# Attention with a token mixer: the last two heads' rows divided while turned, and first products of output blocks moved between the main loop, the ending and the tail

## The chip, the core and the metric

One core of one Trainium2 chip runs the whole program. Its engines are TensorE (PE, with PEld its weight loads), VectorE (DVE), ScalarE (ACT), GpSimd (POOL) and SyncE (SP, which only issues transfers here). The metric is the device time of one execution in microseconds (us), as the median of several runs.

## What is computed

Cut to what matters (`_layernorm`, `_silu`, `_gelu` as usual):

```
xn = layernorm(x)                       # x: 2048 tokens x 512
q, k, v = split(xn @ wqkv)              # 32 heads of 16
s = concat_heads(softmax(q k^T / 4) v) @ wo
h = layernorm(xn)
u = gelu(einsum("bsd,sf->bdf", h, w1) + b1)     # F = 1792
g = silu((einsum("bdf,fs->bds", u, w2) + b2)^T)
out = x + s * g
```

## The kernel before, in words

Matrix operands are kept as an upper and a lower part (`fp32r`), so one product of the reference is three matmuls: upper by upper, upper by lower, lower by upper (`three`, and the three entries in `products`, L1033). Below, "product" means one such matmul over 128 rows.

**Main loop.** After the projections, the loop at L1274 runs in steps of two units, s = 0, 2, ..., 534; NU = 512 and LEAD = 22. For s < 512 a step computes the row maxima of scores (`max_of`: 8 matmuls L532 into 3 PSUM banks, each followed by a VectorE reduction L536); 22 units later it computes the scores again (`score`: 8 matmuls L999, each followed by a ScalarE exponential L1004); two units after that `values` multiplies the probabilities by v (L1015), four heads' columns at a time. Every 16 units `max_rows` turns the maxima into two extra pieces of VectorE work (L551 and L548, L548), popped in the next two steps. Scores and maxima use only 48 or 50 rows of the array, on the lower or upper half of it; so every product that fills the gaps is cut into two halves of 64 rows (`halves`, L1144, matmuls at L1156) that run beside scores and maxima on the other half. How many products a step gets is set by `count` (L1167), and their place in it by `ORDERS` and `WIDE`, written out by hand.

The fill is one long generator: first `mixer` (14 blocks of 48 products with w1, then 16 blocks of 42 with w2), then `rest` (L1023). A mixer block of 42 is spread over eight steps: 6, 6, 5, 5, 5, 5, 5, 5 products; a block of 48 over nine: 6, 6, 6 and six of 5. For the one block whose index equals `SLOW` (4) the divisor is 15 and not 16, and what is left of it in the steady loop is taken as 5, 5, 5, 5, 5, 4, 4, 4. After the mixer, `rest` makes the attention's output products in first parts: for each block b of 128 tokens, nine products over head groups 0 to 2 (`range(ND - 1)`), for b < PARTS = 14. Such a block of nine takes two steps at once (`both_pairs`). Its sum is copied out by ScalarE (`part`, L922), multiplied by the gate g and added to x by GpSimd, and stored to DRAM (`y_d`).

**The ending** is the 12 steps from s = 512 on: no maxima are left, 22 more units of scores are. Scores and the former maxima's banks are one list of seven (L1281), the eighth is `values`'. A half step (`a_half`, L1184) takes up to three products; up to s = 522 only the first half of a step takes any (L1333). The products here are group 3's: three for each of blocks 8 to 13, then three for each of blocks 0 to 7. `finish` (L975) multiplies and adds on VectorE and, for blocks 0 to 7, stores the output. `own` (L831) treats heads 30 and 31 (the last pair), whose sums are never stored to DRAM: for the first 1024 tokens they are divided and moved by DMA into rows 96 to 127 of group 3's operand `oc[3, 0..1]`; `in_halves` reloads partial sums and gates into operands no longer needed, two per step, on SP's queue.

**The tail** is what follows the loop (L1368 on). Blocks 14 and 15 have all their products here, 12 each (`beside`, L1375, handed out by `some`). The last pair's sums of the second 1024 tokens are copied (`ev`, L724), turned by four transposes (L840), inverted (L843), spread wide (L845), turned back (L854), multiplied (L858), split (L859 and L94), and then multiplied with the rows of wo that belong to heads 30 and 31, laid out in a tile of their own (`load_last_w`, `split_last_w`): three products for each of blocks 8 to 15 (L101 to L103). `gated`, `added` and `in_parts` then multiply by the gate, add, and store each block.

Of the kernel before, what the change touches and what calls it, by code (L numbers as in the profile page):

```python
# [21 lines left out]
def tile_attention_token_mixer(ctx, tc, x, wqkv, wo, w1, b1, w2, b2, out):  # L22
# [746 lines left out]
    def divide(m, g, span):  # L769
# [61 lines left out]
    def own(span, ev):  # L831
        rq = sm.tile([P, 4, 4], F32, name="rq", bufs=1)
        wide = el.tile([P, 512], F32, name="t", bufs=4)

        def one(pl=ps_mx, nm="mx", spread=1):

            ps = pl.tile([P, 512], F32, name=nm)
# [6 lines left out]
            for k in range(0, 4, 4 // spread):  # L844
                nc.vector.tensor_copy(  # L845
                    wide.rearrange("p (k j r) -> p k j r", k=4, j=4)[:, k : k + 4 // spread],
                    rq[:, k : k + 4 // spread].unsqueeze(3).to_broadcast([P, 4 // spread, 4, 32]),
                )

        def two(pl=ps_mx, nm="mx", ks=range(4)):  # L850

            ps = pl.tile([P, 512], F32, name=nm)
            for k in ks:
                nc.tensor.transpose(ps[:, k * P : (k + 1) * P], wide[:, k * P : (k + 1) * P], ident)  # L854
            return ps

        def times(ps, of, at):
            nc.vector.tensor_tensor(out=ev[:, at], in0=ps[:, at], in1=ev[:, at], op=OP.mult)  # L858
            nc.scalar.copy(of[:, 0, at], ev[:, at])  # L859

        def lower(of, at):
            sub(nc.vector, of[:, 1, at], ev[:, at], of[:, 0, at])

        if span == QH - 1:
            asides.extend((one, two, times, lower))
            return

        def move_in():
            ps = two()
            of = el.tile([P, 2, 512], F32R, name="uo")  # L870
            times(ps, of, slice(0, 512))
            lower(of, slice(0, 512))
# [7 lines left out]


    last_w = {}

    def load_last_w():
        for c in range(2):
            raw = last_w[c] = wp.tile([P, 4, P], F32, name="raw", bufs=3).rearrange("p a b -> p (a b)")
            nc.gpsimd.memset(raw, 0.0)
            for a in range(2):
                row = 32 * (2 * a + c) + DH * a
                h = H - 2 + a  # L890
                nc.gpsimd.dma_start(raw[row : row + DH, :], wo[DH * h : DH * (h + 1), :])

    def split_last_w():
        for c in range(2):
            raw = last_w[c]
            w = last_w[c] = el.tile([P, 2, 512], F32R, name="uo")
            nc.scalar.copy(w[:, 0, :], raw)
            after(2 + 2 * c, lambda w=w, raw=raw: sub(nc.vector, w[:, 1, :], raw, w[:, 0, :]))


# [6 lines left out]
    PARTS = NB // 2 + 6  # L907
    blocks = list(range(NB // 2, PARTS)) + list(range(NB // 2))

# [39 lines left out]
    def load_out(n):  # L949
        b = blocks[n]  # L950
        y, g = (("xt", "gt"), ("u", "sq"))[n % 2]
        if b < NB // 2:
            ys[b] = el.tile([P, D], F32, name=y)
            nc.sync.dma_start(ys[b], y_d[b])
        gts[b] = el.tile([P, D], F32, name=g)
        nc.sync.dma_start(gts[b], g_d[b])
# [3 lines left out]
    def plan_halves():  # L960

        rows = [oc[g, c][:, m, :].bitcast(F32) for c in range(NC - 1) for g in range(ND - 1) for m in range(2)]
        own = PARTS - NB // 2
        for n in range(own, len(blocks) - 3):
            b = blocks[n]
            in_halves.extend(((ys, b, y_d[b]), (gts, b, g_d[b])))
# [8 lines left out]
    def finish(n, ps):  # L975
        b = blocks[n]
        half = PARTS - NB // 2 <= n < len(blocks) - 3
        r = el.tile([P, D], F32, name="t", bufs=4) if half else gts[b]
        nc.vector.tensor_tensor(out=r, in0=ps, in1=gts[b], op=OP.mult)
        o = ys[b] if b >= NB // 2 else r  # L980
        nc.vector.tensor_tensor(out=o, in0=ys[b], in1=r, op=OP.add)
        if b < NB // 2:
            nc.sync.dma_start(out[b * P : (b + 1) * P, :], r)
        if n + 3 < PARTS - NB // 2:
            load_out(n + 3)
        elif n < PARTS - NB // 2:
            load_out(n + len(blocks) - PARTS + NB // 2)
# [35 lines left out]
    def rest():  # L1023
# [20 lines left out]
        for b in range(PARTS):  # L1044
# [6 lines left out]
        yield from until(lambda: now[0] >= NU and (ND - 1, QH - 1) in divided)  # L1051
        for n in range(3):
            load_out(n)
        plan_halves()
        for n, b in enumerate(blocks):
            if b == 0:
                yield from until(lambda: own_done and (ND - 1, 0) in divided)
# [3 lines left out]
            yield lambda n=n, ps=ps: finish(n, ps), back  # L1061
# [28 lines left out]
    SLOW = 4  # L1090
# [76 lines left out]
    def count():  # L1167
# [10 lines left out]
        return min(6, -(-left // -(-3 * left // (15 if i == SLOW else 16)))) if left > 0 else 0  # L1178
# [95 lines left out]
    for s in range(0, total + 1, 2):  # L1274
# [53 lines left out]
        else:  # L1328


            for i in range(2):

                a_half(*(heads[a][1][2 * i : 2 * i + 2] for a in range(2)), i == 0 or s >= NU + 2 * (PARTS - NB // 2))  # L1333
# [89 lines left out]
    for k in range(5):  # L1423
        if k < 4:
            times(shares[k], of, cols[k])
# [46 lines left out]
```

## Time and profile before

| what | value |
|---|---|
| median of 3 runs | 1624.81 us (1624.67 to 1625.59) |
| the profiled execution: span from its first to its last instruction | 1622.0 us |
| time of the profiled execution around its span | not given; the median stands 2.8 us above the span |
| busy: PE, DVE, ACT, POOL | 1615.0, 1423.3, 1195.1, 561.6 us |

PE is TensorE; its ends are modelled, so "busy" for it is no proof that it is at its peak. A mean of 0.999 of TensorE's full clock was granted. Times in the trace are counted from the span's start: the main loop's steady part runs from about 203 to 1553 us, the ending to 1604, the tail to 1622.

### The profile page before, as it was taken

How to read it: one execution, taken by the hardware profiler on the slowest of the kernel's cores; microseconds unless marked ns; L12 is line 12 of the kernel's file. 1: busy time of each engine (PE TensorE's matmuls, PEld its weight loads, DVE VectorE, ACT ScalarE, POOL GpSimd, SP SyncE). 2: the span in 40 equal slices, each digit the busy share in tenths (PEclk: the TensorE clock that was granted, in tenths of full speed). 3: DMA queues.
4: the chain of work that ended last, by engine and by line, in shares of the span. 5: the costliest groups of instructions: out<-in, count | busy, mean ns of one | idle time of the engine just before them, and what ended most of it. 6: DMA issues, size and time to landing. Idle time of an engine off the chain costs nothing.

```text
span 1622.0 us, 31241 instructions
## 1 busy us (share of the span) xinstructions
PE 1615.0 (100%) x11937; PEld 877.2 (54%) x11937; DVE 1423.3 (88%) x2493; ACT 1195.1 (74%) x2311; POOL 561.6 (35%) x661
## 2 busy tenths in 40 slices
PE   9999999999999999999999999999999999999998
PEld 7888854544555544554554554545544544454544
DVE  7665999999999999999999999999999999999966
ACT  3333477777777777777877787777777778888885
POOL 1224844342244332342333332322222333642430
PEclk9999999999999999999999999999999999999999
DMA  7478441515133141826151522305151515444355
GB/s 237 181 242 204 114 92 41 95 41 75 41 70 73 30 82 34 241 70 108 41 86 38 82 65 40 77 22 76 38 85 37 112 39 84 123 101 130 106 192 192
DMA packets 152402, 155.60 MB, mean 96 GB/s; under 512 B 51564, under 2 KB 110188, under 8 KB 149180
## 3 DMA queue, kind: packets, MB, share of 16 engines
q1 hardware_dynamic: 147964, 152.87, 38.9%
q8 instruction: 94, 1.54, 0.4%
q0 software_dynamic: 4288, 0.73, 0.3%
q14 instruction: 56, 0.46, 0.1%
HBM read 101.86 MB, written 50.58 MB: 94 GB/s over the span
## 4 chain that ended last, share of the span: by engine, by line
PE 98%; DVE 1%; ACT 1%; DMA 0%; SPq 0%; issue 0%; POOL 0%; DVEq 0%
PE av L1015 31%; PE dn L1156 25%; PE sc L999 16%; PE mx L532 13%; PE sc L435 3%; PE dn L671 3%; PE mx L435 2%; PE av L435 1%; PE sc L101 0%; PE sc L103 0%; PE sc L102 0%; ACT prob L1004 0%; DVE mxp L536 0%; PE mx L999 0%; PE dn L1200 0%; PE mx L103 0%
## 5 line engine op out<-in xcount | busy, mean ns | idle before, releaser
L536 DVE TENSOR_REDUCE mxp<-mx 128x1 f32<-128x512 f32 x2026 | 1250.1, 680 | 116.1 <-PE mx L532 85.0
L1004 ACT ACTIVATE prob<-sc 128x512 f32<-128x512 f32 x2004 | 1040.4, 606 | 282.3 <-PE sc L999 117.6
L532 PE MATMUL mx<-big 48*128 48x512 f32 x2026 | 771.1, 418 | 0.1
L999 PE MATMUL sc<-big 50*128 50x512 f32 x2004 | 734.5, 411 | 0.0
L1015 PE MATMUL av<-prob,vp 128*32 128x512 f32 x4096 | 545.6, 604 | 0.3 <-DVE ev L722 0.2
L1156 PE MATMUL dn<-hu,wh 64*128 64x512 f32 x1520 | 508.0, 404 | 0.0
L999 PEld LDWEIGHTS sc<-big 50*128 50x128 f32 x2004 | 355.6, 186 | 230.0 <-ACT prob L1004 205.2
L532 PEld LDWEIGHTS mx<-big 48*128 48x128 f32 x2026 | 356.9, 185 | 187.7 <-DVE mxp L536 168.7
L1156 PEld LDWEIGHTS dn<-hu,wh 64*128 64x128 f32 x1520 | 271.8, 184 | 74.3 <-issue 49.5
L1156 PE MATMUL dn<-hu,wl 64*128 64x512 f32 x762 | 302.4, 397 | 0.0
L1015 PEld LDWEIGHTS av<-prob,vp 128*32 128x32 f32 x4096 | 80.9, 108 | 177.3 <-issue 165.0
L94 POOL TENSOR_TENSOR wl<-raw,wh 128x512 fp32r<-128x512 f32 x124 | 150.9, 1219 | 60.5 <-ACT wh L166 26.9
L1156 PEld LDWEIGHTS dn<-hu,wl 64*128 64x128 f32 x762 | 140.5, 184 | 12.6
L164 POOL CAST wh<-raw 128x512 fp32r<-128x512 f32 x104 | 60.6, 583 | 196.0 <-PE mx L532 76.0
L560 POOL CAST m<-f 16x128 fp32r<-16x128 f32 x31 | 8.7, 280 | 304.0 <-DVE f L548 303.9
L98 POOL DMA_DIRECT2D big<-m x124 | 65.8, 537 | 0.0
L1156 PE MATMUL dn<-wh,hu 64*128 64x512 f32 x168 | 59.7, 408 | 0.0
L621 POOL TENSOR_TENSOR sq<-u 128x512 f32<-128x512 f32 x11 | 11.5, 1041 | 133.8 <-ACT u L615 133.7
L708 POOL TENSOR_SCALAR t<-t 128x512 f32<-128x512 f32 x16 | 23.8, 1489 | 83.4 <-ACT t L705 83.4
L435 PE MATMUL sc<-xt,big 128*128 128x512 f32 x184 | 44.3, 389 | 0.0
L94 POOL TENSOR_TENSOR hu<-hx,hu 128x512 fp32r<-128x512 f32 x16 | 20.4, 1294 | 67.7 <-ACT hu L278 67.7
L671 PE MATMUL dn<-hu,wh 64*128 64x512 f32 x128 | 42.3, 392 | 0.0
(235 smaller groups left out, 1214.9 us busy)
## 6 DMA issues: line engine op xcount, KB each, us to landing
raw<-in_B_w_dram SPq DMA_DIRECT2D x104, 256.0 KB
big<-k_d SPq DMA_DIRECT2D x96, 128.0 KB
big<-q_d SPq DMA_DIRECT2D x96, 128.0 KB
q_d<-sg SPq DMA_DIRECT2D x16, 512.0 KB
k_d<-sg SPq DMA_DIRECT2D x16, 512.0 KB
num_d<-ev SPq DMA_DIRECT2D x30, 256.0 KB
u_d<-uo SPq DMA_DIRECT2D x14, 512.0 KB
hu<-u_d SPq DMA_DIRECT2D x14, 512.0 KB
```

The lines of the kernel that those rows point to most:

```text
L94: eng.tensor_tensor(out=o, in0=a, in1=b.bitcast(F32), op=OP.subtract)
L98: queue.dma_start(dst.bitcast(F32), src.bitcast(F32))
L164: nc.gpsimd.tensor_copy(whs[n][:, :m, :], raws[n][:, :m, :])
L435: nc.tensor.matmul(ps, w[part][:, kd, m], xt[kd][:, z, :], start=w is wh and z == 0 and kd == 0, stop=w is wl and kd == ND - 1,)
L532: nc.tensor.matmul(ps, q[o : o + 48, r * P : (r + 1) * P], k[o : o + 48, c * 512 : (c + 1) * 512], start=True, stop=True,)
L536: nc.vector.tensor_reduce(mxp[u // 16][:, a, r % 8, c : c + 1], ps, axis=AX.X, op=OP.max)
L671: nc.tensor.matmul(ps, w(slice(0, 64)), m(slice(0, 64)), start=first, stop=last)
L708: nc.gpsimd.tensor_scalar(t, t, 1.0, None, op0=OP.add)
L999: nc.tensor.matmul(ps, ks[p][o : o + 50, kb * P : (kb + 1) * P], qs[p][o : o + 50, at : at + 512], start=True, stop=True,)
L1004: nc.scalar.activation(e, ps, AF.Exp, scale=scale)
L1015: nc.tensor.matmul(av[32 * j : 32 * j + 32, :], vps[p][:, kb, 16 * a : 16 * a + 32], prob.pop((t, a, c)), start=kb == 0, stop=kb == NB - 1,)
L1156: made.append(lambda r=r, start=first and a == lead, stop=last and a != lead: nc.tensor.matmul(ps, w(r), m(r), start=start, stop=stop,))
```

## The change

Four things, all in one diff:

1. Blocks 11 and 12 have their nine first products in the ending (interleaved by group: three of block 11, three of block 12, and so on), in the half steps in which blocks 8 to 13 had their three products of group 3. `PARTS` becomes 13, and blocks 13, 14 and 15 have their nine first products in the tail. Blocks 0 to 10 stay in the main loop.
2. Six mixer blocks of w2 (indices 16, 18, ..., 26) get the divisor 15 too: they are spread over nine steps, 5, 5, 5, 5, 5, 5, 4, 4, 4.
3. In the tail, the last pair's rows are divided right after the first turn, while tokens lie on partitions (four multiplications of 128 x 64 into a cleared tile), turned back in four pairs of transposes straight to rows 96 to 127, and written by ScalarE (upper) and VectorE (lower), 32 x 256 each, into rows 96 to 127 of group 3's operand. Group 3 then needs three products for each of blocks 8 to 15, with all 128 rows and the ordinary weights; the special weight tiles, their loads on GpSimd's queue and their splits go.
4. `finish` serves blocks 0 to 7 only; the rows 96 to 127 of the operands are no longer cleared in `divide`, and one tile is cleared at s = 528 instead.

The diff, cut to its core:

```diff
@@ own @@
         if last:
             for c in range(2):
                 made.append(hu.tile([P, 2, 512], F32R, name="hu"))
-                nc.gpsimd.memset(made[c][DH * n :, :, :].bitcast(F32), 0.0)
...
     def own(span, ev):
+        if span == QH - 1:
+            asides.append(ev)
+            return
...
-    def load_last_w():
-    def split_last_w():
...
+    apart = []
+    def clear_apart():
+        apart.append(el.tile([P, 2, 512], F32, name="uo"))
+        nc.gpsimd.memset(apart[0], 0.0)
...
-    PARTS = NB // 2 + 6
-    blocks = list(range(NB // 2, PARTS)) + list(range(NB // 2))
+    PARTS = NB - 3
+    LATE = NB - 5
+    HALVES = 5
...
-    def finish(n, ps):
+    def finish(b, ps):
+        r = el.tile([P, D], F32, name="t", bufs=4) if b < HALVES else gts[b]
         nc.vector.tensor_tensor(out=r, in0=ps, in1=gts[b], op=OP.mult)
+        nc.vector.tensor_tensor(out=r, in0=ys[b], in1=r, op=OP.add)
+        nc.sync.dma_start(out[b * P : (b + 1) * P, :], r)
+        if b + HALVES < NB // 2:
+            load_out(b + HALVES)
...
+        def whole_part(b):
             yield from until(lambda: all((g, b // (NB // QH)) in divided for g in range(ND - 1)))
             ps, back = ps_sc.hold("dn")
             ps = ps[:, :D]
             yield from products(ps, b, range(ND - 1))
             yield lambda b=b, ps=ps: part(b, ps), back
             yield None
-        yield from until(lambda: now[0] >= NU and (ND - 1, QH - 1) in divided)
-        for n in range(3):
-            load_out(n)
+        for b in range(LATE):
+            yield from whole_part(b)
+        yield from until(lambda: now[0] >= NU)
         plan_halves()
-        for n, b in enumerate(blocks):
+        late = [whole_part(b) for b in range(LATE, PARTS)]
+        for n in range(ND - 1):
+            for turn in late:
+                yield from (itertools.islice(turn, 3) if n < ND - 2 else turn)
+        yield from until(lambda: own_done and (ND - 1, 0) in divided)
+        for b in range(NB // 2):
...
-    SLOW = 4
+    SLOW = (4, 16, 18, 20, 22, 24, 26)
...
-        return min(6, -(-left // -(-3 * left // (15 if i == SLOW else 16)))) if left > 0 else 0
+        return min(6, -(-left // -(-3 * left // (15 if i in SLOW else 16)))) if left > 0 else 0
...
-            if s == NU + 4:
-                load_last_w()
+            if s == NU + 16:
+                clear_apart()
...
-            if s == total - 6:
-                split_last_w()
...
     for b in range(PARTS, NB):
         sums[b] = ps_sc.hold("dn")[0][:, :D]
-        for g in range(ND):
+        for g in range(ND - 1):
...
+    some(3)
+    turned = ps_sc.tile([P, 512], F32, name="sc")
+    for k in range(4):
+        nc.tensor.transpose(turned[:, cols[k]], ev[:, cols[k]], ident)
+    some(3)
+    turned = turned.rearrange("p (k j r) -> p k j r", k=4, j=4)
+    for a in range(2):
+        nc.vector.reciprocal(rq[:, :, 2 * a : 2 * a + 2], turned[:, :, 2 * a : 2 * a + 2, 16 - 16 * a])
+    for c in range(2):
+        for a in range(2):
+            j = 2 * a + c
+            nc.vector.tensor_tensor(
+                out=spread[:, c, :, 96 + DH * a : 112 + DH * a], in0=turned[:, :, j, DH * a : DH * a + DH],
+                in1=rq[:, :, j].unsqueeze(2).to_broadcast([P, 4, DH]), op=OP.mult,
+            )
+    back = [ps_sc.tile([P, 512], F32, name="sc") for h in range(2)]
+    def turn_back(h, c):
+        for k in range(2):
+            at = slice((2 * c + k) * P, (2 * c + k + 1) * P)
+            nc.tensor.transpose(back[h][:, at], spread[:, c, 2 * h + k, :], ident)
+    def upper(h, c):
+        nc.scalar.copy(oc[ND - 1, 2 + c][96:, 0, 256 * h : 256 * h + 256], back[h][96:, 256 * c : 256 * c + 256])
+    def lower(h, c):
+        o = oc[ND - 1, 2 + c][96:, :, 256 * h : 256 * h + 256]
+        sub(nc.vector, o[:, 1, :], back[h][96:, 256 * c : 256 * c + 256], o[:, 0, :])
+    half = [NB // 2 + i for i in (0, 1, 4, 2, 3, 5, 6, 7)]
...
+    turn_back(0, 0)
+    some(1)
+    turn_back(0, 1)
+    some(2)
+    for c in range(2):
+        upper(0, c)
+        lower(0, c)
+    product(0)
+    product(1)
+    for c in range(2):
+        turn_back(1, c)
+        upper(1, c)
+    adding = {0: [0], 1: [], 2: [1], 3: [3, 2], 4: [], 5: [5, 4], 6: [6]}
+    for n, more in enumerate((0, 0, 2, 2, 2, 3, 4, 5)):
+        if n > 1:
+            some(more)
+            product(n)
+        if n == 7:
+            in_parts(n)
+            break
+        gated(n)
+        for i in adding[n]:
+            added(i, nc.gpsimd if i in (0, 3, 5) else nc.vector)
+        if n < 2:
+            lower(1, n)
```

## Rows read from the trace of the kernel before

**Rows 1.** The page: busy time of each engine, and the chain's engines.

```profile
PE 1615.0 (100%) x11937; PEld 877.2 (54%) x11937; DVE 1423.3 (88%) x2493; ACT 1195.1 (74%) x2311; POOL 561.6 (35%) x661
...
PE 98%; DVE 1%; ACT 1%; DMA 0%; SPq 0%; issue 0%; POOL 0%; DVEq 0%
```

**Rows 2.** Stretches of the main loop, cut at first value products; columns in the first line.

```profile
core 0: us, PE busy (x) PEld busy (x) DVE busy (x) ACT busy (x) POOL busy (x), PEclk, DMA share, GB/s
762.51:768.04 5.53, 5.53 (x44) 2.79 (x43) 5.38 (x12) 4.23 (x9) 3.01 (x3) 1.00 0.55 128
...
209.31:214.75 5.44, 5.44 (x44) 2.74 (x43) 4.94 (x9) 4.58 (x10) 3.96 (x4) 1.00 1.02 135
225.63:230.83 5.20, 5.20 (x42) 2.64 (x41) 4.70 (x8) 3.88 (x9) 0.00 (x0) 1.00 0.00 0
230.83:236.35 5.52, 5.47 (x42) 2.53 (x40) 5.37 (x12) 4.04 (x9) 0.00 (x0) 1.00 0.01 3
236.35:241.62 5.27, 5.27 (x43) 2.60 (x41) 5.22 (x12) 4.09 (x9) 2.84 (x6) 1.00 0.02 2
...
734.74:778.91 44.17, 44.17 (x343) 22.35 (x341) 40.40 (x70) 35.79 (x70) 17.34 (x21) 1.00 0.60 103
1402.58:1542.73 140.15, 140.01 (x1067) 69.67 (x1067) 131.57 (x226) 118.74 (x233) 62.42 (x62) 1.00 0.44 119
```

**Rows 3.** DVE's timeline inside the steps of four: start, length, line, count.

```profile
232.17 0.22 DVE L551 TENSOR_REDUCE neg<-mxp 128x16 f32<-128x64 f32 x1
232.49 0.41 DVE L548 STREAM_TRANSPOSE f<-neg 32x32 f32<-32x32 f32 x2
...
237.69 0.42 DVE L548 STREAM_TRANSPOSE f<-neg 32x32 f32<-32x32 f32 x2
238.05 4.82 DVE L536 TENSOR_REDUCE mxp<-mx 128x1 f32<-128x512 f32 x8
```

**Rows 4.** Stretches of the ending, columns as in Rows 2.

```profile
1560.97:1564.99 4.02, 4.02 (x32) 1.47 (x31) 1.38 (x2) 4.02 (x9) 2.43 (x5) 1.00 0.59 185
1564.99:1569.25 4.26, 4.09 (x32) 1.47 (x30) 2.08 (x3) 4.26 (x9) 0.14 (x1) 1.00 0.84 292
1592.60:1597.32 4.72, 4.72 (x38) 2.13 (x36) 3.37 (x6) 4.72 (x11) 0.00 (x0) 1.00 0.73 256
```

**Rows 5.** By source line: the part copies and the split of the special weights.

```profile
L922 ACT COPY t<-dn x14: 627/629/654, 1412.1 to 1551.9; 128x512 f32<-128x512 f32 x14
...
L897 ACT CAST uo<-raw x2: 643/646/649, 1593.7 to 1594.2; 128x512 fp32r<-128x512 f32 x2
```

**Rows 6.** ACT's timeline in the ending, with SP's issues of the first half's operand.

```profile
1560.90 0.60 ACT L1004 ACTIVATE prob<-sc 128x512 f32<-128x512 f32 x1
1561.39 0.59 ACT L1004 ACTIVATE prob<-mx 128x512 f32<-128x512 f32 x1
...
1577.03 2.48 SPq L98 DMA_DIRECT2D hu<-uo  x4
```

**Rows 7.** The chain that ended last, in the tail: start, length, what.

```profile
1604.44 1.13 PE dn L1375 x4
1605.57 0.45 PE sc L840 x4
...
1607.75 0.50 PE sc L101
...
1613.80 2.75 PE dn L1375 x12
...
1617.28 0.43 DVE prob L1417
```

**Rows 8.** Groups by line in the tail: count | busy us, mean ns of one.

```profile
L858 DVE TENSOR_TENSOR ev<-sc,ev 128x128 f32<-128x128 f32 x4 | 1.1, 284 | 0.1
L845 DVE COPY t<-rq 128x128 f32<-128x128 f32 x4 | 0.6, 222 | 0.0
```

More of the change, by code (lines that the diff above doesn't have):

```diff
@@ L1 @@
+import itertools
 from contextlib import ExitStack
@@ L843, in one, with move_in @@
                 nc.vector.reciprocal(rq[:, :, 2 * a : 2 * a + 2], turned[:, :, 2 * a : 2 * a + 2, 16 - 16 * a])
[L844 to L853, printed above, removed]
-                nc.tensor.transpose(ps[:, k * P : (k + 1) * P], wide[:, k * P : (k + 1) * P], ident)
[L855 to L869, printed above, removed]
+            nc.vector.tensor_copy(
+                wide.rearrange("p (k j r) -> p k j r", k=4, j=4), rq.unsqueeze(3).to_broadcast([P, 4, 4, 32]),
+            )
+        def move_in():
+            ps = ps_mx.tile([P, 512], F32, name="mx")
+            for k in range(4):
+                nc.tensor.transpose(ps[:, k * P : (k + 1) * P], wide[:, k * P : (k + 1) * P], ident)
             of = el.tile([P, 2, 512], F32R, name="uo")
-            times(ps, of, slice(0, 512))
-            lower(of, slice(0, 512))
+            nc.vector.tensor_tensor(out=ev, in0=ps, in1=ev, op=OP.mult)
+            nc.scalar.copy(of[:, 0, :], ev)
+            sub(nc.vector, of[:, 1, :], ev, of[:, 0, :])
             for a in range(2):
@@ L962, in plan_halves @@
         rows = [oc[g, c][:, m, :].bitcast(F32) for c in range(NC - 1) for g in range(ND - 1) for m in range(2)]
-        own = PARTS - NB // 2
-        for n in range(own, len(blocks) - 3):
-            b = blocks[n]
+        for b in range(HALVES):
             in_halves.extend(((ys, b, y_d[b]), (gts, b, g_d[b])))
@@ L1382, in some @@
         del beside[:n]
-    one, two, times, lower = asides
-    some(4)
-    one(ps_sc, "sc", 4)
+    ev, = asides
+    cols = [slice(k * P, (k + 1) * P) for k in range(4)]
+    spread = apart[0].rearrange("p c (k r) -> p c k r", k=4)
+    rq = sm.tile([P, 4, 4], F32, name="rq", bufs=1)
     some(3)
-    shares = [two(ps_sc, "sc", [k]) for k in range(4)]
-    some(1)
-    of = ks[NP - 1][:, :1024].rearrange("p (a q) -> p a q", a=2)
-    half = [NB // 2 + 4 * c + k for k in range(4) for c in range(2)]
+    turned = ps_sc.tile([P, 512], F32, name="sc")
+    for k in range(4):
+        nc.tensor.transpose(turned[:, cols[k]], ev[:, cols[k]], ident)
[9 more added lines that the diff above has]
+                in1=rq[:, :, j].unsqueeze(2).to_broadcast([P, 4, DH]), op=OP.mult,
+            )
+    back = [ps_sc.tile([P, 512], F32, name="sc") for h in range(2)]
[9 more added lines that the diff above has]
+    half = [NB // 2 + i for i in (0, 1, 4, 2, 3, 5, 6, 7)]
     def product(n):
@@ L1396, in product @@
         if new:
-            sums[b] = (ps_av if n == 2 else ps_sc).tile([P, 512], F32, name="av" if n == 2 else "sc")[:, :D]
-        at = slice(n // 2 * P, (n // 2 + 1) * P)
-        w = last_w[n % 2]
-        three(sums[b], of[:, 0, at], of[:, 1, at], w[:, 0, :], w[:, 1, :], new, True)
+            sums[b] = (ps_av if n == 1 else ps_sc).tile([P, 512], F32, name="av" if n == 1 else "sc")[:, :D]
+        o, at = oc[ND - 1, b // 4], cols[b % 4]
+        for m, w in ((0, 0), (0, 1), (1, 0)):
+            nc.tensor.matmul(sums[b], o[:, m, at], wide[w], start=new and m == 0 and w == 0, stop=m == 1)
     def gated(n):
```

68 lines of the change are left out of this document (9 added, 59 removed).

## The prediction

> **What bounds the kernel now.** I read the page first: PE is busy throughout and the chain that ended last is 98% PE [rows 1]. PE's ends are modelled, so I then cut the main loop into single steps, to see whether a step gets longer with each product in it. It does. A step with five products takes 5.44 us, or 5.53 where VectorE also has a piece of the row maxima [rows 2]. One mixer block of 42 products takes 44.17 us [rows 2]: less five steps of 5.44 and one of 5.53, 11.44 is left for its two steps of six, 5.72 each. So the sixth product costs 0.28 us, close to the 0.23 us that one product takes in a row of them (2.75 us for 12) [rows 7]. TensorE bounds the loop down to five products. But VectorE is close behind: 4.94 of 5.44 us [rows 2]. Below five the question is whose limit comes next, and the change makes 18 steps of four.
>
> The ending was read the same way: 4.02 us a step while half of its half steps take products, 4.72 once all do [rows 4]. In the first kind ScalarE is as full as TensorE (4.02 of 4.02, and 4.26 of a step of 4.26) [rows 4]; an exponential starts every 0.49 us [rows 6], so eight need 3.9. In the second kind PE sets the pace. In the tail the chain is PE's products from 1604.44 us to 1617.28, with a short relay over VectorE and ScalarE between the first turn (1605.57) and the first of the last pair's products (1607.75) [rows 7].
>
> **The counts.** Before: 14 blocks of nine first products in the main loop, 42 products in the ending (14 blocks by three), 24 + 24 in the tail. After: 11 blocks of nine in the main loop, 42 in the ending (18 late ones and 24), 27 + 24 in the tail. The main loop loses 27, the ending keeps its number, half step by half step, the tail gains three. The 24 that vanish are the last pair's separate products.
>
> **Main loop, wide steps.** The stretch of 26 steps, or 13 blocks of nine, takes 140.15 us [rows 2], 10.78 a block. Three go: 3 x 10.78 = 32.34 us saved. The loop has a fixed number of steps, since maxima and scores set it, so these six steps come back elsewhere: as a ninth step in each of six w2 blocks. A step of nothing but scores and maxima is therefore not what is bought; six blocks of 6, 6, 5 x 6 become 5 x 6, 4 x 3.
>
> **Main loop, the nine-step blocks.** Twelve steps of six go: 12 x 5.72 = 68.64 us. Eighteen steps of four come. The trace has three of these, in block 4. The window just before the first full one, without any piece of the maxima, took 5.20 us [rows 2], and that is also 5.44 less one product. The next two took 5.52 and 5.27 [rows 2]; they hold the maxima's pieces, 0.22 + 0.41 us and 0.42 us on VectorE, whose eight reductions then run 4.82 us without a gap [rows 3]: there VectorE was the limit (5.37 of 5.52, 5.22 of 5.27 busy). The pieces come up in steps with s divisible by 16 and in the next one. Counting the starts of the new blocks (232, 266, 300, 334, 368, 402), the steps of four lie at 244 to 248, 278 to 282, 312 to 316, 346 to 350, 380 to 384 and 414 to 418, so three of the 18 hold a piece: 384 and 416 a first one, 418 a second. I take 15 x 5.20 + 2 x 5.52 + 5.27 = 94.31 us. Bounds for a step without a piece: 5.16 as the low end (5.44 less the 0.28 of a sixth product), 5.44 as the high one, where the missing product buys nothing.
> The row says that eight reductions need 4.82 to 4.94 us, so 5.20 leaves them room; the step's sum is TensorE's. The Trainium skill, TensorEngine Tiling (Array Packing), section Performance Considerations (PSUM Bottleneck), speaks against the change: packing the array speeds up the matmuls but not the reading of PSUM, so that the engines that read it may become the limit. By that rule the 18 steps would stay near 5.44 to 5.52 and most of the gain would go (the first rival).
> Main loop together: -32.34 - 68.64 + 94.31 = **-6.67 us** (-7.3 with 5.16, -3.1 with 5.44 throughout). Weight loads and splits, on SP and GpSimd, follow the products and come later, not closer; GpSimd was busy 17.34 of 44.17 us [rows 2]. The divisions follow the mixer, which now ends at s = 468 and not 456; the last of them waits for sums made near the end in either kernel, and is no longer needed before the tail.
>
> **Ending.** PE's sum stays. Added: two copies of a sum by ScalarE at 0.63 us [rows 5], for blocks 11 and 12, at s = 522 and 524, and behind each two GpSimd operations, a store and a reload on SP. Gone: two casts of 0.65 us on ScalarE [rows 5], but in a stretch where PE set the pace (4.72) and they cost nothing; six times two VectorE operations, off the path; GpSimd's two loads, likewise. Of the two copies the first meets a full ScalarE; the second falls where PE needs 4.72 and the exponentials 3.9, which has 0.8 us of room. Second, two banks are held by late blocks through six steps where one was, so scores rotate over five others, not six: a score then waits for the exponential five earlier. Matching four scores against exponentials 0.49 us apart leaves some 0.3 us. Between -0.2 (part of the 0.24 by which one step exceeds 4.02 [rows 4]) and +1.2 (both copies in full) I take **+0.5 us**, nearest to the first copy alone.
> SP: the store of block 12's sum comes at s = 528 and its reload one step later, behind that store's landing; what queues behind is output stores and gate reloads, each with steps to spare, and the sum is needed in the tail, 15 us on. Without that cover one such wait would cost about the 2.5 us for which SP stood at a data wait before [rows 6]. `finish` of block 3 reuses block 12's buffer and must wait for that store; behind it on VectorE are later `finish`es, and scores wait for their bank, but VectorE is idle for 1.3 of each 4.72 us [rows 4]. The moved clears are 0 (GpSimd idle there, [rows 4]).
>
> **Tail.** Three more products: 3 x 0.23 = 0.69 us. Four more transposes at 0.45 / 4: 0.45 us [rows 7]. The relay: before, 12.84 us from 1604.44 to 1617.28 held 48 x 0.23 + 8 x 0.11 = 11.9 us of work, 0.9 idle. After, the turn starts a product earlier (three ahead, not four), and behind it three products (0.69 us) lie over two reciprocals and the first two multiplications. A multiplication of 128 x 64 isn't in the trace: between 0.15 (a spread copy of 128 x 128) and 0.28 (a multiplication of 128 x 128 from PSUM) [rows 8]; I take 0.2, nearer the smaller work. With 0.3 for the reciprocals that is 0.7, covered. The 32 x 256 copy by ScalarE and the VectorE subtraction (at most the 0.63 of [rows 5] and 0.43 of [rows 7]) lie under the three products and the second turn-back, 0.9 us. I leave 0.65 idle, 0.25 less: +0.69 + 0.45 - 0.25 = **+0.9 us**. It can't be below +0.4 (no idle at all is not to be had: the first product of a run shows 0.2 more) and may reach +1.6, where the relay stalls as it did. Behind the last product, `in_parts` is the same.
>
> **Sum.** -6.67 + 0.5 + 0.9 = -5.27 us on a span of 1622.0. The median of the runs stands at 1624.81, 2.8 above that span; I carry that over: 1624.81 - 5.27 = **1619.5 us**, 0.33% faster. A measurement of this kernel can tell about 0.2%, 3.2 us, from no change.
>
> **Rivals.**
> 1. *VectorE takes over in the steps of four.* For it: the two full windows at 5.52 and 5.27, VectorE without a gap. Against: both hold extra pieces. Price: 18 steps at 5.44 to 5.52 give -3.1 to -1.6 in the loop, so 1623.1 to 1624.6 in all. Chance 0.20.
> 2. *Slower: the bank held by the second late block.* If each of the twelve half steps from s = 512 to 522 waits for one more exponential than now (0.49 us [rows 6], or 0.6 with its own start), the ending pays 12 x 0.6 = 7.2 instead of 0.5: -6.67 + 7.2 + 0.9 = +1.4, 1626.2. It decides from 0.48 us a half step. For it: ScalarE is already full there [rows 4]. Against: the 0.3 us of room, and that a bank was at times held twice before. Chance 0.06.
> 3. *It doesn't do what it says:* a block slips by a step, misses its wide pair, and its nine products go to the ending: 9 x 0.23 = 2.1 us there, less 0.9 where two steps go down to VectorE's 4.94 [rows 2] from 10.78: 1620.7. For it: such a pair needs s divisible by four; against: the counts end on s = 468. Chance 0.04.
>
> **Numbers.** Forecast 0.70, with its own range of 1617.5 (low ends of the three parts, and 0.2 for the runs' spread) to 1621.5. With rival 3 that is 0.74; to hold eight in ten the range must go into rival 1, to 1623.6. Faster by over 0.2% (below 1621.6): nearly all of the forecast and rival 3, 0.70. Slower (above 1628.1): the worst of rival 2, 0.03. Within: 0.27.
>
> **What would show it.** Steps of four at 5.2 us away from the maxima's pieces, blocks 16, 18, ... near 48.3 us; 11 wide blocks; part copies of blocks 11 and 12 in the ending, and no growth of its first six steps beyond 1 us; from the last value product to the end of the last product 13.7 us. It is wrong if steps of four read 5.4 or more, if scores wait on exponentials in the ending's first six steps, or if PE shows gaps of half a microsecond after the turn.

## The result, and the profile after

The changed kernel takes 1629.16 us (8 runs, 1628.81 to 1630.32) against 1624.86 (8 runs, 1624.61 to 1625.59): the ratio is 1.0027 [1.0018, 1.0036], so it is slower, by 0.27%. The forecast was 1619.5, its range ended at 1623.6.

The page of the kernel after, with the lines that answer to [rows 1]: TensorE, VectorE, ScalarE and GpSimd are all busy for *less* time than before, and yet the span grew from 1622.0 to 1627.4 us.

```profile
PE 1613.9 (99%) x11890; PEld 874.0 (54%) x11890; DVE 1413.3 (87%) x2474; ACT 1192.2 (73%) x2308; POOL 555.0 (34%) x653
...
PE 98%; DVE 1%; DMA 0%; ACT 0%; SPq 0%; issue 0%; POOL 0%; ACTq 0%
```

To find where that goes, each point of the program was read in both traces, and the time after set against the time before (the main loop ends at the first value product of s = 510, so the border step counts to the ending):

| point | after minus before, us | growth since the point above | predicted growth |
|---|---|---|---|
| steady loop starts | +0.09 | | |
| main loop ends (s = 510) | -3.02 | -3.11 | -6.67 |
| ending ends | -2.20 | +0.82 | +0.5 |
| last product ends | -0.51 | +1.69 | +0.9 |
| outputs landed (SP's first drain at the end) | -0.78 | -0.27 | 0 |
| span ends | +5.4 | +6.2 | 0 |

So all the work of the kernel, its stores included, was done 0.8 us *earlier* than before. What made it slower comes afterwards. A DRAIN is an instruction that stands at the end of each engine's own list. Here are the instructions of the program's end, source line L1462 (L1468 before), by engine: duration in ns as least/median/most, then first and last start in us. After:

```profile
L1462 POOLq DRAIN  x3: 40/106/12181, 1614.4 to 1627.1; - x3
L1462 SPq DRAIN  x3: 7/7/13, 1620.4 to 1626.8; - x3
L1462 DVEq DRAIN  x2: 19/242/464, 1618.0 to 1626.9; - x2
```

The same line of the kernel before:

```profile
L1468 POOLq DRAIN  x3: 46/102/2312, 1613.2 to 1621.8; - x3
L1468 SPq DRAIN  x3: 7/7/13, 1621.2 to 1621.5; - x3
```

And GpSimd's last operations after, from the timeline:

```profile
1612.62 1.62 POOL L1402 TENSOR_TENSOR prob<-big,prob 128x512 f32<-128x512 f32 x1 [3.47 <-issue]
1614.43 1.61 POOL L1402 TENSOR_TENSOR prob<-big,prob 128x512 f32<-128x512 f32 x1 [0.19 <-DVE prob L1398]
```

GpSimd's DRAIN begins with its last addition and took 12.18 us, to 1626.58. The addition itself ended at 1614.43 + 1.61 = 1616.04, so the drain lasted 10.55 us beyond it. Before, the drain ended at 1615.51, 0.99 us after GpSimd's last addition (1614.53), hidden under the last products. After, SP is through at 1620.4 and every engine then waits for GpSimd until 1626.6. The chain on the page doesn't show this: it ends with the last computation, at 1618.45.

The stretches of the main loop and the ending after, which answer to [rows 2, 4] (columns as there): a step before a new block, two mixer blocks (nine steps and eight), two steps of four, the step across the border to the ending, one of its first six steps, and s = 524.

```profile
779.29:785.10 5.81, 5.81 (x44) 2.65 (x43) 5.32 (x9) 5.00 (x11) 0.49 (x1) 1.00 0.01 4
785.10:878.30 93.20, 93.20 (x713) 46.48 (x712) 85.76 (x147) 73.30 (x144) 24.63 (x32) 1.00 0.30 59
817.58:822.83 5.25, 5.25 (x42) 2.67 (x41) 5.00 (x10) 3.90 (x9) 1.22 (x1) 1.00 0.01 2
822.83:828.15 5.32, 5.32 (x42) 2.53 (x40) 5.01 (x10) 4.55 (x10) 1.52 (x2) 1.00 0.00 1
1544.96:1551.89 6.93, 6.71 (x47) 3.26 (x46) 6.27 (x14) 6.44 (x14) 6.63 (x7) 1.00 0.37 89
1554.41:1558.43 4.02, 4.02 (x32) 1.47 (x31) 0.98 (x1) 3.96 (x9) 0.83 (x1) 1.00 0.46 164
1575.94:1580.98 5.04, 5.04 (x36) 2.17 (x34) 0.00 (x0) 5.04 (x12) 3.19 (x3) 1.00 0.51 137
```

Two of these stretches in the kernel before, two blocks of eight steps and the border:

```profile
734.74:823.08 88.34, 88.34 (x683) 44.70 (x681) 80.80 (x139) 70.57 (x137) 29.73 (x37) 1.00 0.35 69
...
1547.97:1554.43 6.46, 6.46 (x47) 3.28 (x45) 5.82 (x12) 6.05 (x13) 6.17 (x7) 1.00 0.15 51
```

A ninth step costs 93.20 - 88.34 = 4.86 us; the forecast had (94.31 - 68.64) / 6 = 4.28. Six times the 0.58 between them is 3.5 us, all that the main loop lacks (3.11 against 6.67).

The tail of the chain after, which answers to [rows 7]: start, length, what.

```profile
1602.24 0.90 PE dn L1341 x3
1603.13 0.45 PE sc L1357 x4
...
1607.41 0.23 PE sc L1374 x2
...
1607.66 0.37 ACT hu L1377
...
1608.08 0.44 PE sc L1374 x2
...
1616.05 0.69 PE dn L1392 x3
...
1618.02 0.43 DVE prob L1410
```

From 1602.24 to the last product's end at 1616.74 it is 14.50 us, where [rows 7] give 12.8. The relay that the prediction worried about (first turn to first turn-back) is short, but there is a new wait between the two later turn-backs.

### The profile page after: what moved, and what is told of

Same layout as the page of the kernel before. It is cut to its first block, busy times and chain, and to the rows that moved or that the text cites. A ratio compares the mean times of both kernels' runs of the same rounds, so it can differ in the third digit from the quotient of the medians.

```text
span 1627.4 us, 31079 instructions
## 1 busy us (share of the span) xinstructions
PE 1613.9 (99%) x11890; PEld 874.0 (54%) x11890; DVE 1413.3 (87%) x2474; ACT 1192.2 (73%) x2308; POOL 555.0 (34%) x653
## 3 DMA queue, kind: packets, MB, share of 16 engines
q0 software_dynamic: 4160, 0.60, 0.3%
## 4 chain that ended last, share of the span: by engine, by line
PE 98%; DVE 1%; DMA 0%; ACT 0%; SPq 0%; issue 0%; POOL 0%; ACTq 0%
PE av L978 31%; PE dn L1123 23%; PE sc L962 17%; PE mx L533 14%; PE sc L436 3%; PE mx L436 2%; PE dn L672 2%; PE av L436 1%; PE dn L673 1%; PE sc L102 0%; PE sc L104 0%; PE sc L103 0%; PE mx L962 0%; PE dn L1341 0%; DMA raw<-in_A_wqkv_dram 0%; PE mx L104 0%
## 5 line engine op out<-in xcount | busy, mean ns | idle before, releaser
L1123 PE MATMUL dn<-wh,hu 64*128 64x512 f32 x132 | 46.9, 408 | 0.0
```

The source lines that it names most:

```text
L1123: made.append(lambda r=r, start=first and a == lead, stop=last and a != lead: nc.tensor.matmul(ps, w(r), m(r), start=start, stop=stop,))
```

## The experiments

Beside each run the kernel before was timed on the same chip: 1624.37 us for the additions, the loads put back and the order for five; 1624.14 for one load, four early loads, six first and the turn-backs; 1625.14 for the kernel before with its loads on SP, for 127 transfers and for no ninth steps; 1624.74 for all three remedies and the large load; 1624.88 for four small loads. The profiled execution of each kernel other than the one before lies 1.7 to 1.8 us above its span (after: 1629.14 and 1627.4).

### GpSimd's drain: is it the late additions?

The additions of the tail were the first suspect: GpSimd makes three after the change, two before. One of them goes to VectorE:

```diff
-            added(i, nc.gpsimd if i in (0, 3, 5) else nc.vector)
+            added(i, nc.gpsimd if i in (0, 3) else nc.vector)
```

> The changed kernel, with the last of GpSimd's three additions in the tail (block 13) on VectorE. In the changed kernel GpSimd's drain at the program's end lasts until 10.5 us after its last addition (1616.04 to 1626.58 us), in the kernel before 1.0 us, though SP had seen every output land at 1620.4. Theory A: the long drain comes with the third addition, which follows the second within 0.2 us; then the drain is short again (about 1 us after the second addition) and the span is 1621.5 to 1622.0. Theory B: the drain lasts a fixed 10.5 us after the last addition in this kernel, whatever that is; it then ends at about 1624.8 and the span is about 1625.5. Theory C: the drain waits for something else than the additions; the span stays at 1627.4.

It took 1626.98 us, 1.0017 [1.0008, 1.0026] of before. The drain has moved with the last addition and is as long:

```profile
L1462 POOLq DRAIN  x3: 46/106/12195, 1612.0 to 1624.7; - x3
```

Its last addition ended at 1613.61, the drain at 1624.16: again 10.55 us beyond. So the delay is fixed and starts at GpSimd's last operation. With all additions on VectorE (`added(i, nc.vector)`) it should be hidden:

> The changed kernel, with all three of GpSimd's additions in the tail on VectorE, so that GpSimd's last instruction is the clearing of a tile at 1583 us. Theories A and B: the drain is over long before the outputs land, and the span is set by VectorE's additions and the outputs: VectorE gets three more additions of 0.69 us, of which it has idle time for about one, so the span is 1621.5 to 1623. Theory C (the drain waits for something else): the span stays near 1627.

1623.42 us, 0.9993 [0.9984, 1.0003]. The drain is still 10.55 us beyond GpSimd's last operation, now the clearing that ended at 1583.17, and it is over at 1593.72, in the ending:

```profile
L1462 POOLq DRAIN  x3: 46/102/12757, 1581.0 to 1621.5; - x3
```

The change also took four loads and two clears from GpSimd (`load_last_w`). This run puts them back, into tiles that nothing reads:

```diff
+            if s == NU + 4:
+                for c in range(2):
+                    spare = wp.tile([P, 4, P], F32, name="raw", bufs=3).rearrange("p a b -> p (a b)")
+                    nc.gpsimd.memset(spare, 0.0)
+                    for a in range(2):
+                        row = 32 * (2 * a + c) + DH * a
+                        h = H - 2 + a
+                        nc.gpsimd.dma_start(spare[row : row + DH, :], wo[DH * h : DH * (h + 1), :])
```

> The changed kernel, with GpSimd's two clears and four loads of rows of wo put back at s = 516, where the kernel before had them (the tiles are not used). Theory D: the drain is long because GpSimd's own DMA queue was last used some 90 us before the end and not 50; then the drain is about 1 us again and the span 1621.5 to 1622. Theories A and B: nothing changes, 1627.4.

1622.85 us, 0.9991 [0.9981, 1.0000], with the additions where the change has them. The drain is 0.99 us beyond the last addition, as before the change:

```profile
L1470 POOLq DRAIN  x3: 46/102/2628, 1614.1 to 1620.8; - x3
```

### Which property of the loads?

One small load (16 x 64, at s = 516), and four of that size far earlier (at s = 300):

```diff
+            if s == NU + 4:
+                spare = sm.tile([16, 64], F32, name="spare", bufs=1)
+                for h in range(1):
+                    nc.gpsimd.dma_start(spare, wo[DH * h : DH * (h + 1), :64])
```

> The changed kernel, with one small load (16 x 64) on GpSimd's queue at s = 516; nothing uses it. With four loads there the drain took 1.0 us beyond the last addition and not 10.5. If any late load on GpSimd's queue will do, the drain is about 1 us again and the span 1621 to 1622. If it takes the four (a count, or the amount), the drain stays at 10.5 us and the span at 1627.

> The changed kernel, with four small loads (16 x 64) on GpSimd's queue at s = 300, some 970 us into the run and followed by the maxima's own moves on that queue up to 1520 us. If the number of GpSimd's DMA issues decides (132 as in the kernel before, and not 128), the drain is about 1 us and the span 1621 to 1622. If what decides is how late the last one is, or what comes behind it, the drain stays at 10.5 us and the span at 1627.

Both keep the drain short: 0.74 us beyond the last addition with one load (1623.33 us, one execution), 0.99 with four early ones (1623.96, one execution). With one load:

```profile
L1466 POOLq DRAIN  x3: 46/106/2374, 1614.8 to 1621.3; - x3
```

Neither run adds a clear, so it is the loads that matter. A load hundreds of us before the end can't matter by being recent: that theory falls. What is left is a count. The issues on GpSimd's queue after (the transfers view: what, count, size, time to landing) add up to 124 + 4 = 128:

```profile
big<-m POOLq DMA_DIRECT2D x124, 4.0 KB, 1.6
big<-ones POOLq DMA_DIRECT2D x4, 16.0 KB, 6.2
```

The kernel before has four more, 132. If the count is the cause, the kernel *before*, with nothing changed but the queue of its four loads, must get slow too:

```diff
-                nc.gpsimd.dma_start(raw[row : row + DH, :], wo[DH * h : DH * (h + 1), :])
+                nc.sync.dma_start(raw[row : row + DH, :], wo[DH * h : DH * (h + 1), :])
```

> The kernel before, with its four late loads of rows of wo issued by SP and not by GpSimd, so that GpSimd issues 128 transfers, as in the changed kernel, and not 132. If the number decides, the drain lasts some 10.5 us beyond GpSimd's last addition (1614.5) here too, so to 1625, and the span is about 1625.7, 3.7 us longer. If something else in the changed kernel decides, the drain stays at 1 us and the span at 1622.

It does: 1628.88 us, 1.0022 [1.0012, 1.0032], with the long drain. This reproduces nearly the whole loss without any part of the change but the loads' place:

```profile
L1468 POOLq DRAIN  x3: 40/106/11867, 1614.6 to 1627.0; - x3
```

Is it exactly 128? One of the four moves of `ones` goes to SP, so that 127 are left:

```diff
-            nc.gpsimd.dma_start(ks[p][row : row + 2, :].bitcast(F32), ones)
+            (nc.sync if p == 0 and a == 0 else nc.gpsimd).dma_start(ks[p][row : row + 2, :].bitcast(F32), ones)
```

> The changed kernel, with one of GpSimd's first four small moves (the rows of ones) issued by SP: 127 transfers on GpSimd's queue and not 128. If 128 itself is what costs (with 129 and 132 it did not), the drain is about 1 us beyond the last addition and the span 1621 to 1622. If any number up to 128 costs, it stays at 10.5 us and the span at 1627.

1629.19 us, 1.0027 [1.0018, 1.0037]; the drain is 12.10 us long:

```profile
L1462 POOLq DRAIN  x3: 40/102/12104, 1614.9 to 1627.5; - x3
```

So 127 and 128 are slow, 129 and 132 are not. Transfers, packets or bytes? Two runs of one execution each separate these. The first adds one large load to those 127:

```diff
+            if s == NU + 4:
+                spare = sm.tile([P, 64], F32, name="spare", bufs=1)
+                nc.gpsimd.dma_start(spare, wo[:P, :64])
```

> The changed kernel with 128 transfers on GpSimd's queue as before, but with one of the four small early moves (rows of ones) issued by SP and a load of 128 rows of 64 put at s = 516 instead, so that the queue carries more packets than with 129 or fewer small transfers (4160 packets with 128, 4192 with 129). If the number of transfers decides, the drain stays at 10.5 us beyond the last addition and the span at 1627. If the number of packets decides, the drain is about 1 us and the span 1621 to 1622.

The expectation's premise was off: the queue carried 4144 packets, fewer than the 4160 of the kernel after and not more, so it excludes only bytes (0.61 MB with a long drain, 0.60 with a short one in the run with one small load), and the idea that any load from DRAM on this queue makes the drain short. It took 1629.59 us:

```profile
L1465 POOLq DRAIN  x3: 46/106/12176, 1614.8 to 1627.5; - x3
```

```profile
q0 software_dynamic: 4144, 0.61, 0.3%
```

The second makes the same 4144 packets out of 129 transfers: three of the moves of `ones` go to SP, four small loads are added.

```diff
-            nc.gpsimd.dma_start(ks[p][row : row + 2, :].bitcast(F32), ones)
+            (nc.gpsimd if p == 1 and a == 1 else nc.sync).dma_start(ks[p][row : row + 2, :].bitcast(F32), ones)
...
+            if s == NU + 4:
+                spare = sm.tile([16, 64], F32, name="spare", bufs=1)
+                for h in range(4):
+                    nc.gpsimd.dma_start(spare, wo[DH * h : DH * (h + 1), :64])
```

> The changed kernel with three of the four moves of `ones` issued by SP and with four small loads (16 x 64) on GpSimd's queue: 129 transfers there, and by the counts of the runs so far (48 packets a move, 32 a load) 4144 packets, as many as in the run with one large load, whose drain was long. If the number of transfers decides, GpSimd's drain at the end lasts to about 1 us beyond its last addition and the span is 1621 to 1622; if the number of packets decides, it lasts to 10.5 us beyond and the span is above 1627.

1622.77 us, and the drain is short:

```profile
L1466 POOLq DRAIN  x3: 46/102/2385, 1614.0 to 1620.7; - x3
```

Its queue, and the issues on it:

```profile
q0 software_dynamic: 4144, 0.56, 0.2%
...
big<-m POOLq DMA_DIRECT2D x124, 4.0 KB, 1.6
spare<-in_A_wo_dram POOLq DMA_DIRECT2D x4, 4.0 KB, 2.8
big<-ones POOLq DMA_DIRECT2D x1, 16.0 KB, 8.1
```

Equal packets, fewer bytes, one transfer more, and the drain falls from 10.54 to 0.75 us beyond the last addition. In one table:

| kernel | transfers | packets | drain beyond GpSimd's last operation, us |
|---|---|---|---|
| 127 | 127 | 4112 | 10.47 |
| after | 128 | 4160 | 10.55 |
| before, its loads on SP | 128 | 4160 | 10.55 |
| one large load | 128 | 4144 | 10.54 |
| four small ones, three moves less | 129 | 4144 | 0.75 |
| one small load | 129 | 4192 | 0.74 |
| before; loads back | 132 | 4288 | 0.99 |

Packets and bytes are excluded; the number of transfers fits every row, with the change between 128 and 129 in this program. One rival is left untested: each kernel with a short drain also has a load of 16 rows on this queue, none with a long one has, and a kernel with 129 transfers and no such load was not run. Against it, the drain follows the number inside both groups: one transfer more adds 0.08 us (127 to 128), three more add 0.25 (129 to 132), and four small loads give 0.75 us among 129 transfers but 0.99 among 132.

The table fits a price for each transfer: 10.47 / 127 and 10.55 / 128 are both 0.082 us, and 0.74 and 0.99 are 9 and 12 times as much. By this estimate the drain goes through the transfers one by one, and with the 129th, 120 of them drop out. What it does with each, and where the next drop comes, no run shows.

### The main loop: does VectorE set the step of four?

This run keeps the four loads (so that its end is that of the run with the loads back) and takes the ninth steps out. The six steps then stand empty at the end of the main loop:

```diff
-    SLOW = (4, 16, 18, 20, 22, 24, 26)
+    SLOW = (4,)
...
-    sizes = [3 * NB] * NF + [3 * NF] * NB + [3 * (ND - 1)] * PARTS
+    sizes = [3 * NB] * NF + [3 * NF] * NB + [3 * (ND - 1)] * LATE
```

> The changed kernel with the four loads (span 1621.0), without the ninth steps: the six w2 blocks take eight steps again, and the six steps gained lie at the end of the main loop with no products in them. If VectorE's eight reductions (4.95 us) and their arrival hold such a step near 5.0 us, six of them cost 30 us against 6 x 4.86 = 29.2 for the ninth steps: the span is 1621 to 1622. If TensorE alone set the pace, a step without products would take 5.44 - 5 x 0.23 = 4.3 us, and the span would be 1617.6.

It took 1627.49 us, 1.0014 [1.0005, 1.0024]; by the ratios that is 3.7 us worse than the run with the loads back. Its span is 1625.5 us, where 1621 to 1622 was expected. What matters is a step without any product, in the windows:

```profile
1528.84:1534.04 5.20, 5.02 (x34) 1.86 (x32) 4.94 (x9) 4.53 (x10) 1.72 (x2) 1.00 0.44 131
```

and VectorE's timeline in it:

```profile
1528.51 4.94 DVE L537 TENSOR_REDUCE mxp<-mx 128x1 f32<-128x512 f32 x8 [0.26 <-PE mx L533]
```

Eight reductions take 4.94 us without a gap, then VectorE waits 0.26 for the first maximum behind the values' products: 5.20 us, with nothing in the gaps of TensorE. So 5.20 is what a step costs *before* the first product is put into it, not the price of four products. The steps of four after (5.25, 5.32) lie close above it. The Trainium skill, TensorEngine Tiling (Array Packing), section Performance Considerations (PSUM Bottleneck), says that packing speeds up the matmuls and not the reading of PSUM; these rows agree (VectorE 4.94 of 5.20).

Are the ninth steps worth having, then? From the first value product of the steady loop to that of s = 512, in the kernel before, in the run with the loads back and in this one:

```profile
209.31:1554.43 1345.12, 1344.92 (x10330) 678.22 (x10329) 1235.29 (x2113) 1065.74 (x2064) 468.94 (x556) 1.00 0.35 75
...
209.80:1551.66 1341.86, 1341.49 (x10277) 673.65 (x10276) 1235.70 (x2115) 1062.82 (x2062) 459.56 (x548) 1.00 0.34 73
...
209.94:1555.07 1345.13, 1343.27 (x10274) 673.62 (x10273) 1236.02 (x2111) 1063.64 (x2060) 459.52 (x548) 1.00 0.35 75
```

With six empty steps the loop gains nothing, with the ninth steps 3.3 us: that is what they are worth. The rest of the 4.4 us between the two spans, some 1.0, arises in the ending and the tail; why was not pursued.

### The main loop: the order at the border

Each nine-step block begins with a step of five, and the window before it grew to 5.81 us, where [rows 2] have 5.44. For a block that begins with six there is an order of its own in `BEGIN`; this run gives blocks that begin with five the like:

```diff
-    BEGIN = {6: ("DDDDDDsmsmsmsm", "msmsmsmsDDDDDD", 0, 7)}
+    BEGIN = {6: ("DDDDDDsmsmsmsm", "msmsmsmsDDDDDD", 0, 7), 5: ("DDDDDsmsmsmsm", "msmsmsmsDDDDD", 0, 7)}
```

> The changed kernel, with an order of its own for the first step of a block that begins with five products: the value products come first in it, as they do for a block that begins with six. In the changed kernel the window at the border into a nine-step block takes 5.81 us against 5.44 for other windows of five products. If the border's 0.37 us comes from the order, these windows fall to about 5.45 and the six blocks give back 6 x 0.37 = 2.2 us of span. If it comes from ScalarE's copy of the finished block's sum between the exponentials, they stay at 5.8.

1631.62 us, 1.0044 [1.0029, 1.0059]: worse. The border takes 4.24 + 7.41 = 11.65 us, where it took 5.81 and 5.44, 11.25, in the kernel after; six such borders are 2.4 us. From the start of the steady loop to s = 510 this run lost 2.2 us against the kernel after.

```profile
779.40:783.64 4.24, 4.24 (x35) 1.67 (x33) 3.74 (x7) 3.44 (x8) 0.51 (x1) 1.00 0.00 0
783.64:791.05 7.41, 7.41 (x55) 4.00 (x53) 6.45 (x11) 6.31 (x14) 3.85 (x4) 1.00 0.47 147
```

So the order alone is no remedy. The next run begins the nine-step blocks with six instead (6, 5, 5, 5, 5, 4, 4, 4, 4), and keeps the four loads:

```diff
+        if new_block[0] and i in SLOW[1:]:
+            return 6
```

> The changed kernel with the four loads of the earlier run (span 1621.0), and the six nine-step blocks spread as 6, 5, 5, 5, 5, 4, 4, 4, 4. If the 0.58 us by which a nine-step block exceeds its sum lie mostly at the border (5.81 us where a block begins with five, because two sums hold banks while scores go on), the border's excess of 0.3 to 0.4 us goes in each of six, and the span falls by about 1.8 us to 1619.2. If they lie in the steps of four, a fourth such step adds to them and the span stays or grows, 1621 to 1622.

1621.76 us, 0.9994 [0.9975, 1.0013]. The interval is wide by one execution of 1637.26 us, in which TensorE's mean granted clock was 0.949; the other nine end at 1622.00. Its two-block period is 92.99 us against 93.20, and the border holds one product more in the same 4.28 + 6.98 = 11.26:

```profile
779.09:783.37 4.28, 4.28 (x35) 1.69 (x33) 3.79 (x7) 3.48 (x8) 0.52 (x1) 1.00 0.00 0
783.37:790.35 6.98, 6.98 (x56) 3.99 (x54) 6.12 (x11) 6.31 (x13) 3.85 (x4) 1.00 0.42 135
783.37:876.36 92.99, 92.99 (x715) 46.86 (x713) 85.55 (x147) 73.47 (x143) 24.72 (x32) 1.00 0.29 60
```

Against before its main loop gains 4.5 us from the start of the steady loop on, 0.8 more than the run with the loads back and 1.4 more than the kernel after: a gain, but its span of 1620.1 us is short of the 1619.2 that was expected.

### The tail: the second turn-back

`upper(1, 0)` reads the bank that the transposes of `turn_back(1, 1)` write, and in the kernel after it is issued first. Both turn-backs go ahead of it, again with the loads back:

```diff
     for c in range(2):
         turn_back(1, c)
+    for c in range(2):
         upper(1, c)
```

> The changed kernel with the four loads (span 1621.0), and in the tail both pairs of transposes of the second half issued before ScalarE's two copies. In the changed kernel the second pair waits for the copy of the first, which reads the same bank: 0.67 us from the first pair's end (1607.41) to the second's (1608.08). If that wait is part of the tail's excess, the end of the last product comes 0.4 us sooner and the span is 1620.6; if other work fills it, nothing changes.

1621.99 us, 0.9986 [0.9976, 0.9995]. The four transposes run without a wait, and from the first `beside` to the end of the last product it is 1615.68 - 1601.87 = 13.81 us, 0.69 less than after, and the span is 1620.5 (1620.6 expected):

```profile
1601.87 0.90 PE dn L1349 x3
...
1607.04 0.44 PE sc L1382 x4
...
1614.99 0.69 PE dn L1400 x3
```

### All three remedies

One small load on GpSimd, six first, and both turn-backs together, with everything else of the change kept:

> The changed kernel with what the runs showed: one small late load on GpSimd's queue (129 transfers), blocks of nine steps begun with six products, and both pairs of transposes of the tail's second half before ScalarE's copies. If the three effects add (4.5 to 6 us for the drain, 1.1 for the borders as measured at the main loop's end, 0.7 for the transposes), the span is about 1619.7, and the time some 4 us (0.25%) under the kernel before's in the same call. If they overlap, it is 1620.5 to 1621.5.

1621.65 us (11 runs, 1621.16 to 1622.41), 0.9980 [0.9971, 0.9989]. It beats both kernels. Its span of 1619.9 us is that of three effects that add (1619.7 expected), but the time is 3.1 us under the kernel before's, not 4. The drain is hidden:

```profile
L1469 POOLq DRAIN  x3: 46/106/2377, 1613.1 to 1619.6; - x3
```

## Why the prediction was wrong

**The end of the program** turned the sign. The step that failed is "GpSimd's two loads, likewise" (off the path), together with "Behind the last product, `in_parts` is the same": the loads (four transfers, not two) were costed at nothing because no computation waited for them, and the sum stopped at the last product. Their price was that the queue fell from 132 to 128 transfers and GpSimd's drain grew by 9.6 us, of which 6.4 became visible: 1627.4 against 1621.0 in the spans without and with the loads. Nothing in the profile of before shows this drain as a bound, but it does show a drain of 2.3 us on GpSimd that the prediction never read. With the loads back the ratio is 0.9991: without this step a gain of 0.09% was left, where 0.33% was forecast, and the terms below took the rest.

**The nine-step blocks**, forecast at +4.28 us each, measured +4.86. The product's price was taken as constant, "5.44 less one product". From six products to five it is 0.28 us, from five to four 0.12 to 0.19, and from four to none at most 0.12, since VectorE's eight reductions and the wait behind the values make 5.20. "5.20 leaves them room; the step's sum is TensorE's" was the wrong reading: the 0.26 us that it took for room is the wait behind the values. So 5.16, the low end, wasn't to be had, and the first rival was right in its mechanism, wrong in its size: the steps didn't stay near 5.44 to 5.52. The rest of the 0.58 is the border to a block that begins with five (5.81 against 5.44), which the sum didn't have at all: it priced steps, and not their neighbours. Wide blocks (-32.34) and the steps of six (-68.64) account for their part: with 4.86 in place of 4.28 the loop's sum is -3.2, and -3.11 was measured.

**The ending**: +0.82 against +0.5, inside its bounds. The second rival was wrong: s = 512 to 522 takes the same time as before, step by step (4.02 where [rows 4] have 4.02), with two banks held. What it does cost lies elsewhere. At the border, 6.93 against 6.46, a score waits 0.18 us for an exponential behind ScalarE's copy of the last main-loop sum. At s = 524, "0.8 us of room" failed: ScalarE is busy 5.04 of 5.04 us with its exponentials, the copy of block 12's sum and what the step before had left.

```profile
1550.76 0.49 PE L962 MATMUL sc<-big 50*128 50x512 f32 x1 [0.18 <-ACT prob L967]
...
1578.89 0.76 ACT L895 COPY t<-dn 128x512 f32<-128x512 f32 x1
```

One reading there was wrong, though no sum used it: the 2.48 us of [rows 6] are four issues in a row, not a wait of SP for data.

**The tail**: +1.69 against +0.9, just beyond its bound of +1.6. The three products and the transposes cost what was said, and so did the first relay. "The 32 x 256 copy ... lie under the three products and the second turn-back" failed for the second pair of tokens: the turn-back can't cover the copy when it writes the bank that the copy reads. That wait is 0.67 us of the 0.79 missing (1607.41 to 1608.52 for four transposes that take 0.44).

**The time around the span**: the 2.8 us carried over set one execution's span against the median of others. In the profiled executions of all other kernels here it is 1.7 to 1.8, and in those of before beside the runs 1.7 to 1.9, but for six with 2.3 to 2.4. So the profiled execution of before was probably 0.4 to 1 us short of its median (its own time isn't given); the prediction took the difference for a constant.

**The third rival** (a block slips) didn't happen: eleven blocks were wide, and blocks 11 and 12 were in the ending.

## What to carry to other kernels

Follow the span to its very end, past the last computation: read each engine's drain there, and ask of every transfer that is removed from a queue what else its queue does, not only who waits for the data. In this kernel one small load more on GpSimd's queue was worth some 6 us (1623.3 against 1629.2). A step's price per product holds only down to the next engine's floor, and the way to find that floor is a step with nothing in its gaps. A transpose that writes the bank that a copy reads can't cover that copy.

## What the runs showed of the hardware that was not expected

GpSimd's drain at the end of the program lasts 10.5 us beyond its last operation in seven kernels with 127 or 128 transfers on its queue, and 0.7 to 1.0 us in those with 129 or 132; packets (4144 either way) and bytes don't decide. Within either group it grows by 0.08 us a transfer. It starts with the last operation, however early that is, so it is hidden when GpSimd stops some 10.5 us before the outputs have landed. The Trainium skill, DMA: Bandwidth & Descriptors, section SWDGE vs HWDGE vs iDMA, says that GpSimd's own processors make the descriptors of the transfers it issues; no run here shows whether that is what the drain waits for.

An addition on GpSimd and one on VectorE disturb each other, and only the one that begins second pays. GpSimd's last two additions took 1.62 and 1.61 us, where the first of the tail took 1.28; both began inside an addition of VectorE's, which kept its 0.68. VectorE's addition that began inside GpSimd's last took 0.90:

```profile
1614.20 0.68 DVE L1402 TENSOR_TENSOR prob<-big,prob 128x512 f32<-128x512 f32 x1
1614.96 0.69 DVE L1398 TENSOR_TENSOR prob<-dn,hu 128x512 f32<-128x512 f32 x1
1615.68 0.90 DVE L1402 TENSOR_TENSOR prob<-big,prob 128x512 f32<-128x512 f32 x1
```

The extra time is what is left of the first one, less 0.13 us: 0.33 with 0.45 left (1614.43 in 1614.20 to 1614.88), 0.22 with 0.35 left (1615.68 in 1614.43 to 1616.04). In the tails of the traces here the 41 pairs of additions with more than that left follow this within 0.01 us. VectorE's multiplication from PSUM inside GpSimd's addition (1614.96) kept its length. No run tried the pair by itself.
